# Source order on every engine, and a gate whose weight is the stationary operand

## The chip, the core and the metric

The kernel runs on one core of a Trainium2 chip. The metric is device time in microseconds (us) of one execution; before the change the median of three runs is 2077.51 us (2077.18 to 2080.61). Five engines work side by side, each through its own queue of instructions in the order in which the program was built: TensorE (PE, with its weight load shown as PEld), VectorE (DVE), ScalarE (ACT), GpSimd (POOL) and SyncE (SP), which here issues the DMAs. An engine that waits for a semaphore holds everything behind it in its queue.

## The reference

Three layers, one after the other, on 2304 tokens of 512 features:

```python
# attention: 4 batches, 8 heads, 576 positions, 64 features a head
q_s = exp(q - max(q, -1)); q_s /= sum(q_s, -1) + 1e-9
k_s = exp(k - max(k, 2));  k_s /= sum(k_s, 2) + 1e-9
x = (q_s @ (k_s^T @ v)).reshape(2304, 512)
# MLP: 512 -> 2048 -> 512
h = x @ w_in;  x = maximum(0.01 * h, h) @ w_out
# gate and Sinkhorn: 8 experts
P = exp(x @ w_gate - max)
for _ in range(8):
    P /= P.sum(1) + 1e-9;  P /= P.sum(0) + 1e-9;  P *= N / E
# dense mixture of experts, 512 -> 1024 -> 512 each
out = sum over e of P[:, e] * (maximum(x @ w1[e], 0) @ w2[e])
```

## The kernel before, in words

**Numbers.** Every fp32 product is emulated: an operand is split into a rounded part *hi* (a copy to fp32r on ACT) and a rest *lo* (a subtraction on DVE, or on POOL), and each product is three matmuls, hi·hi, hi·lo and lo·hi.

**MLP.** It runs in four phases of four hidden units of 128 each (`NPH`, `PU`); in a phase six blocks of 384 tokens (`NB`) pass, and each block takes the four units one after the other. That is 96 steps s. `first(s)` (L174) issues 12 matmuls into a bank `ph`, two leaky relus on ACT (`hh`, the hi part, L188, and `g`, L189) and on DVE the lo part of `hh` (L190). `second(s)` (L192) issues the 12 matmuls into the four `y` banks. At the end of a block the banks go into `acc` by four copies on ACT in phase 0 (L209), by four adds on DVE later (L211); the next block's first `y` matmul writes the same banks and waits for them. The pool of `hh` holds two tiles and that of `g` one, so that `hh` of step s+2 takes the tile that the `y` matmuls of step s read.

**Weights.** The MLP's weights arrive as 64 bit floats in half units of 512 KB (`raw`, three buffers) and `prep_half` (L126) turns each into hi and lo: an absolute value on ACT (L134), five integer and float operations on DVE (L136 to L146), a cast on ACT (L144), two operations on POOL (L148, L149); then it loads the next. The eight half units of a phase go to `wa` or to `wb_t` in turn.

**Gate.** After a block's last phase `gate_block` (L305) multiplies `acc` in plain fp32: 12 matmuls a block (24 in the trace) that hold a 128x128 piece of `acc` still and move the 8 columns of the gate's weight, into `pg`; a copy puts the logits into `lg`. `balance` (L320) takes the maximum (`pmx`, `pmb`) and runs the eight Sinkhorn rounds, each with one small matmul (`pcs`) between DVE operations (L336 to L347).

**Experts.** Three super-blocks of 768 tokens, 32 groups each, 96 groups. A group forms seven half-size products instead of eight (`pa` to `pd`, 6 matmuls each, L451) and then 36 matmuls of an earlier group's output (`e`, L464). `x_sums` (L418) prepares a super-block's seven sums of tokens on DVE and ACT, and splits them.

**What sets the order.** The source is a list of half steps: `half_step(t)` (L590) runs the tasks planned with `at(t, ...)`, advances those that are under way, then issues `first` or `second` (or a seventh of a group), then advances the tasks that asked for `PE_NEXT`. In the kernel before this is only the order of issue: the framework's scheduler then orders every engine's queue by its own estimate of what is ready, with the order of the source as a priority, and it may put a later step's operation ahead of an earlier one.

Of the kernel before, what the change touches and what calls it, by code (L numbers as in the profile page):

```python
# [15 lines left out]
P = 128  # L16
# [6 lines left out]
def kernel(  # L23
# [44 lines left out]
    US = 4 * DM  # L68
    HX = KC // 2 * BLK

    const = ctx.enter_context(tc.tile_pool(name="const", bufs=1))
    hp_ = ctx.enter_context(tc.tile_pool(name="h", bufs=2))
    sk_p = ctx.enter_context(tc.tile_pool(name="sk", bufs=2))
# [8 lines left out]
    def r32(ap):  # L82
        return ap.bitcast(F32)
# [82 lines left out]
    def bank(name):  # L166
        pool, tag = spare[0]
        spare.append(spare.pop(0))
        return pool.tile([P, 512], F32, tag=tag, name=name)
# [22 lines left out]
    def second(s):  # L192
        ph, b, u, beg, end = steps[s]
        if beg:
            for c in range(KC):
                y_t[c] = ps_y.tile([P, 512], F32, tag=f"y{c}", name=f"y{c}_{s}")[:, :BLK]
        assert (u, 1) in ready, (s, u)
        wh, wl = unit(u)[:, 1, 0, :], unit(u)[:, 1, 1, :]
        h = h_t.pop(s)
        for c in range(KC):  # L200
            cs = slice(c * P, (c + 1) * P)
            mm(y_t[c], wh[:, cs], h[:, 0, :], beg, False)
            mm(y_t[c], wh[:, cs], h[:, 1, :], False, False)
            mm(y_t[c], wl[:, cs], h[:, 0, :], False, end)
        if end:
            a = acc[b].rearrange("p (c n) -> p c n", c=KC)
            for c in range(KC):
                if ph == 0:
                    nc.scalar.copy(a[:, c, :], y_t[c])  # L209
                else:  # L210
                    nc.vector.tensor_tensor(a[:, c, :], y_t[c], a[:, c, :], op=ALU.add)  # L211
            if ph == NPH - 1:
                active.append([gate_block(b), PE_NEXT])


    k_t, v_t = {}, {}
# [85 lines left out]
        ready.add(("x", i))  # L302


    def gate_block(b):  # L305
        a = acc[b].rearrange("p (c n) -> p c n", c=KC)
        pg = bank(f"pg{b}")[:, : TB * E].rearrange("p (t e) -> p t e", e=E)
        for t in range(TB):
            for c in range(KC):
                mm(pg[:, t, :], a[:, c, t * P : (t + 1) * P], wg_t[:, c, :], c == 0, c == KC - 1)  # L310
        nc.scalar.copy(lg[:, b * TB : (b + 1) * TB, :], pg)
        ready.add(("gate", b))
        return
        yield

    mrow = const.tile([P, 1], F32, name="mrow")
    mall = const.tile([1, 1], F32, name="mall")
# [100 lines left out]
    def x_sums(sb):  # L418

        b = [  # L420
            acc[2 * sb + t].rearrange("p (k c n) -> p k c n", k=2, c=KC // 2)[:, k]
            for k in range(2)
            for t in range(2)
        ]
        b11, b12, b21, b22 = b
        t1 = later["mo"].tile([P, KC // 2, BLK], F32, tag="s", name=f"t1_{sb}", bufs=1)

        def sub(o, x, y):
            nc.vector.tensor_tensor(o, x, y, op=ALU.subtract)

        def both(name, a):
            split(xt(name)[:, 0], xt(name)[:, 1], a)()
            ready.add(("xt", sb, name))

        sub(t1, b12, b11)
        sub(b12, b22, b12)
        yield
        both("B11", b11)
        both("B22", b22)
        yield  # L440
        sub(b22, b22, t1)
        both("T2", b22)
        both("T1", t1)
        yield
        both("T3", b12)
        both("B21", b21)
        yield
        sub(b21, b21, b22)
        both("T4", b21)
# [211 lines left out]
    for ph in range(1, NPH - 1):  # L661
        for n, (f, half) in enumerate(halves):
            at(H2 * ph + 3 + 9 * n // 2, prep_half, PU * (ph + 1) + f, half)
    at(H2 * (NPH - 1) - 4, open_pairs)
    T3 = H2 * (NPH - 1)
    at(T3 + 8, pair0)
    at(T3 + 34, x_sums, 0)
    END = 2 * NS
    at(END + 2, balance)

    nc.vector.memset(ones, 1.0)
    nc.scalar.activation(mrow, ones[:, :1], AF.Exp)
# [74 lines left out]
```

## Time and profile before

| | |
|---|---|
| median of three runs | 2077.51 us |
| the profiled execution | 2077.42 us, with a span of 2075.6 us (1.82 us lie outside the span) |
| PE busy | 2024.7 us, 98% of the span |
| PEld, DVE, ACT, POOL busy | 1850.2, 1303.4, 794.1, 508.3 us |
| mean granted clock of PE | 0.987 of 2.4 GHz |
| attention and MLP | up to about 554 us |
| experts | about 554 to 2075.6 us, 15.7 us a group |

A page of the profile gives the busy time of each engine and the chain of work that ended last; its trace can be read as a timeline, by lines, by waits and by stretches of time. With PE at 98% the place to look is where PE is not busy, and where its clock is at the lower of its two levels (0.50 in the rows is 1.2 GHz).

### The profile page before, as it was taken

The page shows a single profiled execution, that of the slowest core. Times are in us where ns is not written, and L with a number is a line of the kernel's source. Part 1 is how long each engine was busy: PE and PEld are TensorE (multiplying, and loading weights), DVE is VectorE, ACT ScalarE, POOL GpSimd, SP SyncE. Part 2 cuts the span into 40 slices and gives each one's busy share as a digit, 9 for nine tenths or more (in the row PEclk, how much of TensorE's full clock was granted, in tenths as well). Part 3 has the DMA queues.
Part 4 walks back from the last instruction along what each step waited for, and adds up shares of the span by engine and source line. Part 5 has one row for each costly group of instructions (what it writes and reads, how often), then busy time and mean ns, then how long its engine had stood idle before and what let it go on. Part 6 is the DMA issues. An engine that isn't in the chain of part 4 may idle for free.

```text
span 2075.6 us, 26519 instructions
## 1 busy us (share of the span) xinstructions
PE 2024.7 (98%) x10447; PEld 1850.2 (89%) x10447; DVE 1303.4 (63%) x1899; ACT 794.1 (38%) x1342; POOL 508.3 (24%) x492
## 2 busy tenths in 40 slices
PE   7898798999999999999999999999999999999999
PEld 6898798999988988988988898898888889889887
DVE  8826826234486666666675666666676666666664
ACT  6644322223343343333344333343344433333431
POOL 5604404001121222222222212212212222222220
PEclk9999899999999999999999999999999999999999
DMA  6402202000121221221221211211213212212210
GB/s 239 151 7 74 89 3 89 1 1 1 42 81 41 82 82 41 82 82 41 82 97 57 81 64 59 82 56 67 82 41 112 81 41 81 82 41 82 82 41 31
DMA packets 65453, 138.57 MB, mean 67 GB/s; under 512 B 4656, under 2 KB 4656, under 8 KB 65328
## 3 DMA queue, kind: packets, MB, share of 16 engines
q1 hardware_dynamic: 65328, 136.87, 19.3%
q8 instruction: 82, 1.34, 0.3%
q14 instruction: 43, 0.35, 0.0%
HBM read 132.14 MB, written 4.72 MB: 66 GB/s over the span
## 4 chain that ended last, share of the span: by engine, by line
PE 86%; DVE 6%; issue 5%; ACT 1%; DMA 1%; POOL 1%; SPq 0%; POOLq 0%; ACTq 0%; DVEq 0%
PE e L172 38%; PE pa L172 9%; PE pc L172 9%; PE pd L172 9%; PE y L172 7%; PE ph L172 6%; PE pb L172 5%; DVE ca L140 1%; DVE ca L136 1%; DVE hh L190 1%; PE pg L172 1%; PE px L172 1%; DVE ca L137 1%; DVE raw L146 1%; PE pkv L172 1%
## 5 line engine op out<-in xcount | busy, mean ns | idle before, releaser
L172 PE MATMUL e<-wb_t,xs 128*128 128x512 f32 x3456 | 823.0, 395 | 0.2 <-DVE xs L498 0.2
L172 PEld LDWEIGHTS e<-wb_t,xs 128*128 128x128 f32 x3456 | 647.0, 188 | 149.6 <-DVE xs L498 0.7
L404 POOL TENSOR_TENSOR s<-pair 128x256 f32<-128x256 f32 x96 | 74.3, 774 | 1276.3 <-DMA pair<-in_w 703.8
L491 DVE SCALAR_TENSOR_TENSOR acc<-e,pm,acc 128x512 f32<-128x512 f32 x264 | 193.3, 745 | 104.9 <-PE e L172 102.3
L498 DVE SCALAR_TENSOR_TENSOR xs<-c,xs 128x384 fp32r<-128x384 f32 (+1 forms) x192 | 185.0, 982 | 84.2 <-ACT xs L497 81.1
L172 PE MATMUL pa<-xs,wa 128*128 128x384 f32 x1152 | 231.3, 335 | 2.2 <-ACT c L523 2.2
L172 PE MATMUL pc<-xs,wa 128*128 128x384 f32 x1152 | 230.8, 334 | 0.0
L172 PE MATMUL pd<-xs,wa 128*128 128x384 f32 x1152 | 230.6, 334 | 0.0
L497 ACT ACTIVATE xs<-c 128x768 fp32r<-128x768 f32 x192 | 126.6, 681 | 235.3 <-PE e L172 214.7
L172 PEld LDWEIGHTS pa<-xs,wa 128*128 128x128 f32 x1152 | 203.4, 188 | 11.5 <-ACT c L523 3.1
L172 PEld LDWEIGHTS pd<-xs,wa 128*128 128x128 f32 x1152 | 202.4, 188 | 0.0
L172 PEld LDWEIGHTS pc<-xs,wa 128*128 128x128 f32 x1152 | 202.3, 188 | 0.0
L190 DVE TENSOR_TENSOR hh<-g,hh 128x384 fp32r<-128x384 f32 x96 | 68.3, 712 | 187.6 <-ACT g L189 187.5
L398 DVE TENSOR_TENSOR wa<-s,wa 128x768 fp32r<-128x768 f32 x96 | 91.9, 957 | 105.0 <-ACT wa L397 102.8
L397 ACT CAST wa<-s 128x768 fp32r<-128x768 f32 x96 | 80.1, 835 | 174.4 <-POOL s L407 150.6
L513 DVE TENSOR_TENSOR c<-c 128x384 f32<-128x384 f32 x96 | 53.9, 562 | 135.3 <-ACT c L533 135.3
L172 PE MATMUL y<-hh,wa 128*128 128x384 f32 x576 | 119.8, 358 | 15.8 <-DVE acc L211 5.4
L172 PE MATMUL y<-hh,wb_t 128*128 128x384 f32 x576 | 118.6, 356 | 13.8 <-DVE hh L190 5.1
L523 ACT COPY c<-pa 128x384 f32<-128x384 f32 x96 | 46.2, 481 | 215.5 <-PE pa L172 164.9
L172 PEld LDWEIGHTS y<-hh,wa 128*128 128x128 f32 x576 | 108.0, 200 | 18.7 <-DVE hh L190 6.2
L172 PEld LDWEIGHTS y<-hh,wb_t 128*128 128x128 f32 x576 | 108.4, 202 | 16.6 <-DVE hh L190 6.4
L398 DVE TENSOR_TENSOR wa<-pair,wa 128x1024 fp32r<-128x1024 f32 x96 | 119.6, 1246 | 3.2 <-PE y L172 2.8
(106 smaller groups left out, 2515.5 us busy)
## 6 DMA issues: line engine op xcount, KB each, us to landing
pair<-in_w SPq DMA_DIRECT2D x192, 512.0 KB, 4.9
raw<-in_wm SPq DMA_DIRECT2D x32, 512.0 KB, 3.8
v<-in_vt SPq DMA_DIRECT2D x16, 320.0 KB, 4.7
k<-in_kt SPq DMA_DIRECT2D x16, 288.0 KB, 4.2
out<-acc SPq DMA_DIRECT2D x18, 256.0 KB, 2.0
acc<-in_q SPq DMA_DIRECT2D x5, 768.0 KB, 5.9
acc<-in_q SPq DMA_DIRECT2D x3, 256.0 KB, 5.2
wg_t<-in_wg SPq DMA_DIRECT2D x1, 16.0 KB, 8.9
```

Of the source, the lines that this page charges most:

```text
L136: nc.vector.tensor_scalar(af, af, EXP_MIN, EXP_MAX, op0=ALU.max, op1=ALU.min)
L137: nc.vector.tensor_scalar(a, a, 3, 0x3FFFFFFF, op0=ALU.logical_shift_left, op1=ALU.bitwise_and)
L172: nc.tensor.matmul(o, a, b, start=start, stop=stop, **more)
L190: nc.vector.tensor_tensor(hh[:, 1, :], g, r32(hh[:, 0, :]), op=ALU.subtract)
L397: nc.scalar.copy(hi, a)
L398: return lambda: nc.vector.tensor_tensor(lo, a, r32(hi), op=ALU.subtract)
L404: nc.gpsimd.tensor_tensor(s[:, 0], a21, a22, op=ALU.add)
L491: nc.vector.scalar_tensor_tensor(a, y, scale, a, op0=ALU.mult, op1=ALU.add)
L497: nc.scalar.activation(o[:, 0], p, AF.Relu)
L498: nc.vector.scalar_tensor_tensor(o[:, 1], p, 0.0, r32(o[:, 0]), op0=ALU.max, op1=ALU.subtract)
L513: add = lambda o, x, y: nc.vector.tensor_tensor(o, x, y, op=ALU.add)
L523: nc.scalar.copy(c1, bk[0])
```

## The change

There are four edits. The scheduler is switched off, so that every engine's queue is in the order of the source (`manual_schedule`). The gate is turned round: `acc` is split into hi and lo (into the part of `xs` that held the attention's result for that block, which no one reads any more), the weight becomes the stationary operand with its hi and lo parts side by side (16 columns, `wgs`), 8 matmuls move 384 tokens each into a 16x384 result `pg`, which is split again (`gs`, hi on ACT, lo on DVE), and six small matmuls with `sel`, two identity blocks summed, turn it back to tokens by experts (`pt`) and add the two halves of the weight. The first temporary of `x_sums` takes a tile of the pool `hh` for super-blocks 1 and 2. `balance` starts three half steps later. Line numbers of the kernel after are higher by 2 up to the gate, by 30 to 31 behind it.

```diff
--- before.py
+++ after.py
@@ -68,6 +68,8 @@
     US = 4 * DM
     HX = KC // 2 * BLK
 
+
+    ctx.enter_context(tc.manual_schedule())
     const = ctx.enter_context(tc.tile_pool(name="const", bufs=1))
     hp_ = ctx.enter_context(tc.tile_pool(name="h", bufs=2))
     sk_p = ctx.enter_context(tc.tile_pool(name="sk", bufs=2))
@@ -210,7 +212,7 @@
                 else:
                     nc.vector.tensor_tensor(a[:, c, :], y_t[c], a[:, c, :], op=ALU.add)
             if ph == NPH - 1:
-                active.append([gate_block(b), PE_NEXT])
+                active.append([gate_block(b), None])
 
 
     k_t, v_t = {}, {}
@@ -302,16 +304,44 @@
         ready.add(("x", i))
 
 
+
+    gx = wa[:, PU * US - 2 * DM :]
+    wgs = gx[:, : KC * 2 * E].rearrange("p (c e) -> p c e", c=KC)
+    sel = gx[: 2 * E, KC * 2 * E :][:, :E]
+    gs = gx[: 2 * E, -2 * BLK :].rearrange("p (l n) -> p l n", l=2)
+
+    def gate_weight():
+
+
+        nc.scalar.copy(wgs[:, :, :E], wg_t)
+        nc.vector.tensor_tensor(wgs[:, :, E:], wg_t, r32(wgs[:, :, :E]), op=ALU.subtract)
+        nc.vector.tensor_tensor(
+            sel, ident[: 2 * E, :E], ident[: 2 * E, E : 2 * E], op=ALU.add
+        )
+
     def gate_block(b):
-        a = acc[b].rearrange("p (c n) -> p c n", c=KC)
-        pg = bank(f"pg{b}")[:, : TB * E].rearrange("p (t e) -> p t e", e=E)
+
+        for k in range(2):
+            ks = slice(k * XS // 2, (k + 1) * XS // 2)
+            hi, lo = (xs[:, (2 * b + l) * XS : (2 * b + l + 1) * XS][:, ks] for l in range(2))
+            nc.scalar.copy(hi, acc[b][:, ks])
+            nc.vector.tensor_tensor(lo, acc[b][:, ks], r32(hi), op=ALU.subtract)
+            if k == 0:
+                yield
+        yield PE_NEXT
+        pg = bank(f"pg{b}")[: 2 * E, :BLK]
+        for c in range(KC):
+            for l in range(2):
+                mm(pg, wgs[:, c, :], xb(b, l)[:, c, :], c + l == 0, c + l == KC)
+        nc.scalar.copy(gs[:, 0], pg)
+        nc.vector.tensor_tensor(gs[:, 1], pg, r32(gs[:, 0]), op=ALU.subtract)
+        yield PE_NEXT
+        pt = bank(f"pt{b}")[:, : TB * E].rearrange("p (t e) -> p t e", e=E)
         for t in range(TB):
-            for c in range(KC):
-                mm(pg[:, t, :], a[:, c, t * P : (t + 1) * P], wg_t[:, c, :], c == 0, c == KC - 1)
-        nc.scalar.copy(lg[:, b * TB : (b + 1) * TB, :], pg)
+            for l in range(2):
+                mm(pt[:, t, :], gs[:, l, t * P : (t + 1) * P], sel, l == 0, l == 1)
+        nc.scalar.copy(lg[:, b * TB : (b + 1) * TB, :], pt)
         ready.add(("gate", b))
-        return
-        yield
 
     mrow = const.tile([P, 1], F32, name="mrow")
     mall = const.tile([1, 1], F32, name="mall")
@@ -423,7 +453,8 @@
             for t in range(2)
         ]
         b11, b12, b21, b22 = b
-        t1 = later["mo"].tile([P, KC // 2, BLK], F32, tag="s", name=f"t1_{sb}", bufs=1)
+        pool, tag, bufs = (hp_, "hh", 2) if sb else (later["mo"], "s", 1)
+        t1 = pool.tile([P, KC // 2, BLK], F32, tag=tag, name=f"t1_{sb}", bufs=bufs)
 
         def sub(o, x, y):
             nc.vector.tensor_tensor(o, x, y, op=ALU.subtract)
@@ -662,11 +693,12 @@
         for n, (f, half) in enumerate(halves):
             at(H2 * ph + 3 + 9 * n // 2, prep_half, PU * (ph + 1) + f, half)
     at(H2 * (NPH - 1) - 4, open_pairs)
+    at(H2 * (NPH - 1) + 2, gate_weight)
     T3 = H2 * (NPH - 1)
     at(T3 + 8, pair0)
     at(T3 + 34, x_sums, 0)
     END = 2 * NS
-    at(END + 2, balance)
+    at(END + 5, balance)
 
     nc.vector.memset(ones, 1.0)
     nc.scalar.activation(mrow, ones[:, :1], AF.Exp)
```

On PE at the first gate, before: `ph78` is the first matmul of step 78, `y0_76` to `y3_76` the banks of the block that begins at step 76.

```order
L172 MATMUL ph78_3864<-xs_81,wb_t_1680 128x384 x12
L172 MATMUL pg0_3882<-wg_t_72,acc0_75 128x8 x12
L172 MATMUL y0_76_3897<-hh76_3808,wb_t_1680 128x384 x3
L172 MATMUL y1_76_3898<-hh76_3808,wb_t_1680 128x384 x3
L172 MATMUL y2_76_3899<-hh76_3808,wb_t_1680 128x384 x3
L172 MATMUL y3_76_3900<-hh76_3808,wb_t_1680 128x384 x3
L172 MATMUL ph79_3915<-xs_81,wb_t_1680 128x384 x12
L172 MATMUL y0_76_3897<-hh77_3838,wb_t_1680 128x384 x3
L172 MATMUL y1_76_3898<-hh77_3838,wb_t_1680 128x384 x3
```

And of the kernel after, same place on PE:

```order
L174 MATMUL ph79_3910<-xs_83,wb_t_1682 128x384 x12
L174 MATMUL pg0_3928<-xs_83,wa_84 16x384 x8
L174 MATMUL y0_76_3892<-hh77_3843,wb_t_1682 128x384 x3
L174 MATMUL y1_76_3893<-hh77_3843,wb_t_1682 128x384 x3
L174 MATMUL y2_76_3894<-hh77_3843,wb_t_1682 128x384 x3
L174 MATMUL y3_76_3895<-hh77_3843,wb_t_1682 128x384 x3
L174 MATMUL pt0_3952<-wa_84 128x8 x6
L174 MATMUL ph80_3960<-xs_83,wb_t_1682 128x384 x12
```

`pg0` still stands between a `ph` and a `y`, one step later, with 8 matmuls of 384 columns for 12 of 8; behind the next `y` come the six `pt0` matmuls, ahead of `ph80`.

What stands on ACT there in the kernel after (`wa<-pg0` is the hi part of the gate's result):

```order
L427 CAST wa_84<-pair0_3663 128x1024
L427 CAST wa_84<-s0_3866 128x768
L190 ACTIVATE hh79_3923<-ph79_3910 128x384
L191 ACTIVATE g79_3924<-ph79_3910 128x384
L336 CAST wa_84<-pg0_3928 16x384
L343 COPY lg_75<-pt0_3952 128x24
L190 ACTIVATE hh80_3973<-ph80_3960 128x384
L191 ACTIVATE g80_3974<-ph80_3960 128x384
```

The split of `pg0` stands behind `hh79` and `g79`, and the copy of the logits behind it.

On ACT at the end of block 5 of phase 0, before, where `acc5<-y..` are the copies that free the `y` banks and `ca` is the first operation of a half unit's preparation:

```order
L188 ACTIVATE hh24_1913<-ph24_1900 128x384
L189 ACTIVATE g24_1914<-ph24_1900 128x384
L134 ACTIVATE ca8_1_2215<-raw8_1_2031 128x512
L134 ACTIVATE ca10_0_2291<-raw10_0_2103 128x512
L209 COPY acc5_80<-y0_20_1834 128x384
L209 COPY acc5_80<-y1_20_1835 128x384
L144 CAST wa_82<-ca8_1_2215 128x512
L209 COPY acc5_80<-y2_20_1836 128x384
L188 ACTIVATE hh25_1959<-ph25_1946 128x384
L189 ACTIVATE g25_1960<-ph25_1946 128x384
L209 COPY acc5_80<-y3_20_1837 128x384
L144 CAST wa_82<-ca10_0_2291 128x512
```

And after:

```order
L146 CAST wb_t_1682<-ca7_0_1882 128x512
L136 ACTIVATE ca6_1_1927<-raw6_1_1877 128x512
L190 ACTIVATE hh25_1961<-ph25_1948 128x384
L191 ACTIVATE g25_1962<-ph25_1948 128x384
L146 CAST wb_t_1682<-ca6_1_1927 128x512
L136 ACTIVATE ca7_1_1969<-raw7_1_1922 128x512
L211 COPY acc5_82<-y0_20_1836 128x384
L211 COPY acc5_82<-y1_20_1837 128x384
L211 COPY acc5_82<-y2_20_1838 128x384
L211 COPY acc5_82<-y3_20_1839 128x384
L190 ACTIVATE hh26_2007<-ph26_1994 128x384
L191 ACTIVATE g26_2008<-ph26_1994 128x384
```

The preparations of phase 2's half units (`ca8` to `ca10`), which stood ahead of and between the copies, are gone from here; the copies now stand behind `ca7_1`, in one piece, ahead of `hh26`.

On DVE at the end of super-block 0, before (`t1_1` and the operations on `acc2`, `acc3` belong to `x_sums`, `wa<-s32` prepares group 32, `c1_31` and `c2_31` are sums of group 31):

```order
L398 TENSOR_TENSOR wa_82<-s32_8273,wa_82 128x768
L498 SCALAR_TENSOR_TENSOR xs_81<-c1_30_8152,xs_81 128x384
L498 SCALAR_TENSOR_TENSOR xs_81<-c2_30_8151,xs_81 128x768
L491 SCALAR_TENSOR_TENSOR acc0_75<-e14_0_8220,pm_74,acc0_75 128x512
L429 TENSOR_TENSOR t1_1_8328<-acc3_78,acc2_77 128x768
L398 TENSOR_TENSOR wa_82<-pair32_8207,wa_82 128x1024
L491 SCALAR_TENSOR_TENSOR acc0_75<-e14_1_8236,pm_74,acc0_75 128x512
L429 TENSOR_TENSOR acc3_78<-acc3_78 128x768
L491 SCALAR_TENSOR_TENSOR acc0_75<-e14_2_8251,pm_74,acc0_75 128x512
L513 TENSOR_TENSOR c1_31_8270<-pb_31_8266,c1_31_8270 128x384
L398 TENSOR_TENSOR xs_81<-acc2_77,xs_81 128x768
L398 TENSOR_TENSOR xs_81<-t1_1_8328,xs_81 128x768
```

And after:

```order
L460 TENSOR_TENSOR acc3_80<-acc3_80 128x768
L544 TENSOR_TENSOR c1_31_8329<-pd_31_8327,c1_31_8329 128x384
L529 SCALAR_TENSOR_TENSOR xs_83<-c1_31_8329,xs_83 128x384
L428 TENSOR_TENSOR xs_83<-acc2_79,xs_83 128x768
L428 TENSOR_TENSOR xs_83<-acc3_80,xs_83 128x768
L522 SCALAR_TENSOR_TENSOR acc1_78<-e14_3_8404,pm_76,acc1_78 128x512
L428 TENSOR_TENSOR wa_84<-pair32_8266,wa_84 128x1024
L460 TENSOR_TENSOR acc3_80<-acc3_80,t1_1_8387 128x768
L428 TENSOR_TENSOR xs_83<-acc3_80,xs_83 128x768
L428 TENSOR_TENSOR xs_83<-t1_1_8387,xs_83 128x768
L522 SCALAR_TENSOR_TENSOR acc1_78<-e14_4_8425,pm_76,acc1_78 128x512
L428 TENSOR_TENSOR wa_84<-s32_8332,wa_84 128x768
```

`wa<-s32`, the last of what group 32's second product reads, stands ahead of all of `x_sums` before. After, it stands behind seven of the operations of `x_sums` (the first, `t1_1`, is in the row ahead of those shown) and behind `wa<-pair32`.

## Rows read from the trace of the kernel before

**Rows 1.** Stretches of the span: length, busy us (instructions) by engine, clock, DMA.

```profile
core 0: us, PE busy (x) PEld busy (x) DVE busy (x) ACT busy (x) POOL busy (x), PEclk, DMA share, GB/s
0.00:67.10 67.10, 53.81 (x305) 48.28 (x305) 60.26 (x107) 43.61 (x98) 42.55 (x39) 0.90 0.65 224
67.10:110.90 43.80, 38.93 (x231) 36.89 (x230) 33.59 (x89) 28.36 (x66) 21.97 (x21) 0.92 0.40 127
...
174.12:249.25 75.13, 57.26 (x265) 54.22 (x265) 69.78 (x87) 29.62 (x59) 44.76 (x30) 0.86 0.35 113
...
320.80:342.07 21.27, 14.72 (x73) 13.78 (x73) 20.40 (x26) 6.60 (x13) 11.97 (x9) 0.92 0.39 124
...
553.95:619.40 65.45, 62.80 (x336) 56.05 (x336) 54.77 (x119) 29.24 (x48) 18.62 (x17) 1.00 0.23 76
619.40:2046.55 1427.15, 1425.30 (x7090) 1275.67 (x7090) 948.51 (x1288) 554.51 (x841) 343.60 (x356) 1.00 0.20 68
```

**Rows 2.** Timeline of PE, 183 to 345 us: start, length; in brackets idle before, releaser.

```profile
187.65 3.91 PE L172 MATMUL y<-hh,wa 128*128 128x384 f32 x12 [2.81 <-ACT acc L209]
...
214.66 1.79 PE L172 MATMUL y<-hh,wb_t 128*128 128x384 f32 x6 [3.80 <-ACT acc L209]
...
245.60 3.85 PE L172 MATMUL y<-hh,wb_t 128*128 128x384 f32 x12 [4.02 <-DVE acc L211]
...
338.49 3.75 PE L172 MATMUL y<-hh,wa 128*128 128x384 f32 x12 [5.35 <-DVE acc L211]
```

**Rows 3.** Short stretches, columns as in rows 1; the sixth number is the clock.

```profile
215.28:222.11 6.83, 5.92 (x18) 5.09 (x18) 6.80 (x11) 4.13 (x9) 4.52 (x3) 0.50 0.27 84
227.40:228.30 0.90, 0.04 (x2) 0.03 (x1) 0.90 (x2) 0.00 (x0) 0.82 (x2) 1.00 0.17 68
...
461.04:464.45 3.41, 3.41 (x12) 3.41 (x12) 0.00 (x0) 0.14 (x1) 0.00 (x0) 0.50 0.00 0
```

**Rows 4.** Chain that ended last, at the first gate: start, length, what.

```profile
458.39 2.58 PE pg L172 x24
460.96 3.75 PE y L172 x12
464.71 2.08 PE ph L172 x12
```

**Rows 5.** Timeline of all engines just ahead of the first gate.

```profile
454.02 2.25 PE L172 MATMUL y<-hh,wb_t 128*128 128x384 f32 x12
...
454.75 2.12 DVE L211 TENSOR_TENSOR acc<-y,acc 128x384 f32<-128x384 f32 x4 [1.18 <-PE y L172]
...
456.60 0.48 ACT L188 ACTIVATE hh<-ph 128x384 fp32r<-128x384 f32 x1
...
456.98 0.49 ACT L189 ACTIVATE g<-ph 128x384 f32<-128x384 f32 x1
457.64 0.55 DVE L190 TENSOR_TENSOR hh<-g,hh 128x384 fp32r<-128x384 f32 x1
```

**Rows 6.** Waits of the whole run: us in total, times, longest.

```profile
ACT hh L188 <- PE y L172: 178.3, 62, 3.6
```

**Rows 7.** Instructions by line: busy us, mean ns; idle before, releaser.

```profile
L491 DVE SCALAR_TENSOR_TENSOR acc<-e,pm,acc 128x512 f32<-128x512 f32 x264 | 193.3, 745 | 104.9 <-PE e L172 102.3
...
L398 DVE TENSOR_TENSOR wa<-pair,wa 128x1024 fp32r<-128x1024 f32 x96 | 119.6, 1246 | 3.2 <-PE y L172 2.8
...
L513 DVE TENSOR_TENSOR c<-pb,c 128x384 f32<-128x384 f32 x96 | 53.3, 555 | 48.4 <-PE pb L172 48.4
...
L398 DVE TENSOR_TENSOR xs<-acc,xs 128x768 fp32r<-128x768 f32 x18 | 17.5, 984 | 1.4 <-PE ph L172 1.2
```

**Rows 8.** Chain that ended last, at the end of super-block 0.

```profile
1037.48 1.04 PE pa L172 x6
...
1040.60 8.40 PE e L172 x36
...
1057.51 4.67 PE e L172 x20
```

## The prediction

> **What bounds the kernel now.** I read the stretches first: their PE column shows where PE is not full. From 619 us on it is full, 1425.3 of 1427.2 us at full clock [rows 1], so the experts are bound by PE and source order can only lose there. What can be gained lies in four earlier stretches: PE is busy for 53.8 of 67.1 us, 38.9 of 43.8, 57.3 of 75.1 and 14.7 of 21.3, each with a clock under 1 [rows 1]. A pair of `ph` and `y` costs 4.2 us at full clock (12 matmuls in 2.08 us [rows 4], twice). The 265 matmuls of the third stretch are 11 pairs or 46.3 us, so 28.8 of its 75.1 us are lost; the 73 of the fourth are 3 pairs or 12.6 us, so 8.7 are lost. Next the timeline of PE says what ended the idle time: the copies and adds that free the `y` banks [rows 2], on engines that were then preparing weights (DVE is busy for 69.8 of the 75.1 us [rows 1]). Last I read the clock. The 3.80 us of idle are followed by 6.8 us at 1.2 GHz, whereas at 227.4 us PE is idle for 0.9 us and stays at 2.4 [rows 3]. Twelve matmuls at the lower level took 3.75 us for 2.08 [rows 4], so each drop costs 1.7.
>
> **The change part by part** (after minus before, against the profiled execution's 2077.42 us: a span of 2075.6 and 1.82 outside it; the median of the runs is 2077.51, 0.09 more).
>
> *Start, 0 to 110.9 us.* DVE is busy for 60.3 of the first 67.1 us [rows 1], and its operations there are needed in either order. But the scheduler also does work of the following 44 us early, preparations and softmax pieces. Source order leaves them in their place, so PE should fill 67 to 111 (4.9 us of idle and about 3.5 of lost clock to win, 8% of 43.8). Against that, the first `ph` comes 3 to 6 us later, since pieces of later tasks stand on DVE ahead of the last operation that it needs. I take −5, from −12 to +5.
>
> *111 to 174 us.* PE is full there before; source order brings a few short stalls: +1 (0 to +5).
>
> *Phase 0 to 1, 174 to 249 us.* The scheduler brings phase 2's preparations forward into this stretch, back to back with phase 1's. After, only the eight of phase 1 stand there, some two half steps apart. Two waits remain. The copies of block 4's banks stand on ACT behind `hh21` and a cast that waits for DVE: about 1.9 us. Those of block 5 stand behind `ca7_1`, which waits for a load that in turn waits for POOL to free a buffer: about 5.9. With one to three drops of the clock at 1.7, 9.5 to 13 us are lost for 28.8. That is −17; if nothing waits for loads −24, if more blocks do −8.
>
> *Phases 1 to 3 up to the gate, 249 to 458 us.* The 8.7 us of 321 to 342 go with the crowd of preparations. New is that a block's four adds, 2.12 us on DVE [rows 5], stand behind the lo part of the next `hh` and a preparation's operations; before, they ran ahead of it. The next block's `y` then waits 1.3 us in one block and 2.0 in another of each of phases 1 and 2 (6.6), fourteen other blocks about 0.17 (2.4), and a drop of the clock may follow: +1 (−3 to +5).
>
> *Gate.* Before, a block's gate is 2.58 us on PE [rows 4]. After, eight matmuls of 384 columns at 2.08/12 = 0.173 take 1.4 and the six of `pt` some 0.6 (at 2.58/24 each), 2.0 altogether: 0.6 less, if nobody waits. But `pt0` reads `gs`, whose split stands on ACT behind `hh79` and `g79`. `hh79` takes the tile that `y` of step 77 reads, so it starts only when that `y` has ended. The timeline shows just this wait before: `y` starts at 454.02, takes 2.25, and `hh` starts at 456.60, 0.33 behind its end [rows 5]; ACT spends 178 us so in all [rows 6]. Behind `pg0` PE has just that `y`, and then `pt0`: from the end of `y`, 0.33 for `hh`, 0.87 to `g`'s end (456.60 to 457.47 [rows 5]), about 0.4 for the split's hi, 0.5 for its lo and 0.6 for `pt`: 2.7 us in which PE does next to nothing. A block costs 1.4 + 2.7 = 4.1 for 2.58, so five blocks lose 7.6; the sixth stands among the experts. Lost clock is worth 4.6 in all before (three of six `y` behind a gate are slow, the first with 3.75 [rows 4]); after, each wait of some 2 us may bring 1.7, 0 to 8.5 in all, and I take the same as before. Together +7.6 (+2.6 to +12).
>
> *Balance, 554 to 619 us.* Before, PE is idle for 2.65 us there [rows 1], since the scheduler slides the expert matmuls under each step of the chain. After, the eleven small matmuls (`pt5`, `pmx`, `pmb` and eight `pcs`) have fixed places. The longest waits: `pmx` stands behind a maximum that waits on ACT for `lg`, itself behind a relu and a cast, 2.8; `pcs1` behind a DVE row with one 1.25 and several 0.55 operations of the group [rows 7] and the round's own, 5.9; five more of 0.3 to 1.4, 3.6 together. 12.3 us and two drops of the clock at 1.7 give 15.7, less 2.65 is 13.0; the second drop is unsure, and I take +12 (+7 to +16).
>
> *Ends of super-blocks 0 and 1.* A group is 7 × 1.04 + 8.40 = 15.68 us [rows 8]; at the first end 16.91 pass between two equal points, 1040.60 to 1057.51 [rows 8], so 1.2 are lost. After, from `t1_1` to `wa<-s32` DVE has eight operations of about 0.97, one of 1.25, two of 0.75 and two of 0.55 [rows 7]: 11.6 us, less a little overlap, from some 9.6 us into group 31 on (its four sums and `wb_t<-pair31` come first). So `wa<-s32` is there at 21.1, and the second product of group 32, which would end at 15.68 + 2 × 1.04 = 17.8, ends at 21.9. The splits that follow, T4 last, hold the copy that frees bank `pa` until about 26.4; three more products then end at 29.5 for 23.0. That is 6.5 less 1.2, or 5.3, and up to 8.7 with two drops of the clock; 7 each, +14 (+10 to +18).
>
> *Steady groups, tail.* Walked in source order, DVE and ACT (948.5 and 554.5 of 1427 us [rows 1]) have what PE needs in time: 0.
>
> Sum: −5 + 1 − 17 + 1 + 7.6 + 12 + 14 = +13.6, so 2091.0 us.
>
> **A rule on the clock.** The rows show drops behind idle of 3.80 us and none behind 0.9 [rows 3], and one behind the gate's matmuls without idle [rows 4]. The Trainium skill ("TensorE: Matmul & The Clock Gate", "A second HAM failure mode: psum-queue depth-cycling") says that frequent short idles of TensorE between groups of matmuls can be enough to make the clock swing. The trace agrees only in part: no drop stands at the 0.9 us. By that rule the many short waits that source order adds would cost clock too, which is the third rival.
>
> **The rivals.**
> 1. *Faster: preparations spread over the half steps stall nobody.* It decides in 174 to 249 us: if loads arrive ahead of `ca7_1`, the stretch loses under 5 us, −24 for −17, and with the start at −12 and 249 to 458 at −3, the same mechanism, the first half gives −38. Against the costs at their middle, 7.6 + 12 + 14 = 33.6, that is −4 (2073); at their lower ends, 19.6, −18 (2059). For it: the idle there is crowding, DVE 93% busy [rows 1]. Against: `ca7_1`'s wait stands ahead of the bank's copies in the order. I put it at 2066.
> 2. *Cancelled: the gate's wait doesn't occur.* If `gs` is split before `y` of step 77 ends, five blocks give 5 × 0.6 = 3.0, and the 4.6 of clock may go too: −5 in place of +7.6, the sum is +1.0, and the time 2078 (2071 with balance and the ends of super-blocks near their lower ends as well). For it: `pg0` is done early. Against: two `hh` tiles and the row of 178 us [rows 6].
> 3. *Much slower: every wait of 1 us or more takes the clock down.* About 14 waits (four in phases 1 and 2, five at the gate, five in balance) at 1.7 are 24 us, of which 8 are in the sum (4.6 at the gate, 3.4 in balance): +30, or 2107. For it: the slow `y` behind the gate without idle [rows 4]. Against: 227.4 us [rows 3].
>
> **How the numbers follow.** The forecast's own range, its terms not all at one end, is 2082 to 2103, with a chance of 0.48. The first rival has 0.22, the second 0.16, the third 0.14. A time within 0.2% (4.2 us, about what a measurement of this kernel can tell) of 2077.5 is no change. Faster: 0.20 of the first rival and 0.04 of the second, 0.24. Same: 0.02 and 0.11, 0.13. Slower: the rest, 0.63. The range is 2063 to 2109, with about a tenth beyond each end.
>
> **What would show it.** Right: in the new profile PE's idle before `y` between 174 and 249 us is cut to a few us; `pt` has 2 us of idle ahead of it in five blocks, released by DVE; `pcs` and `pmx` have idle ahead in the first four groups; two groups are some 6 us longer than 15.68. Wrong: the first `ph` more than 8 us later than before, or earlier than it, a steady group unlike 15.68 us, no idle ahead of `pt`, or a mean clock under 0.98.

## The result, and the profile after

The kernel after takes 2102.44 us (median of four runs, 2099.86 to 2104.33) against 2078.03 beside it: slower, with a ratio of 1.0109 (95% interval 1.0095 to 1.0122). Its profiled execution has a span of 2100.8 us, 25.2 more than before. The prediction was 2091.0 us within 2063 to 2109: the right side and within the range, but 13.6 us forecast for the 24 measured.

The stretches of the kernel after, with the columns of [rows 1]; cut at the first matmul of steps 8 and 20, inside steps 32 and 77, at the first group and at the seventh:

```profile
0.00:102.50 102.50, 81.75 (x496) 74.53 (x496) 74.78 (x133) 57.81 (x135) 46.82 (x44) 0.90 0.54 187
102.50:175.13 72.63, 70.19 (x453) 68.17 (x453) 30.09 (x65) 37.69 (x87) 16.88 (x16) 1.00 0.06 21
175.13:240.94 65.81, 56.91 (x298) 55.98 (x298) 46.36 (x67) 25.80 (x55) 30.70 (x20) 0.90 0.25 73
240.94:439.07 198.13, 192.22 (x1082) 189.03 (x1081) 82.64 (x162) 54.78 (x119) 46.27 (x32) 1.00 0.14 43
439.07:552.01 112.94, 102.63 (x544) 95.91 (x542) 45.99 (x71) 34.09 (x68) 3.12 (x4) 0.94 0.00 1
552.01:649.80 97.79, 88.26 (x437) 78.12 (x436) 71.25 (x144) 39.92 (x65) 17.85 (x23) 0.95 0.20 65
```

PE idles for 10.3 us in the fifth and 9.5 in the sixth. Before, it was full at the gate, and 2.65 us were idle in the first groups [rows 1]. Lengths of the same work in both kernels, from the starts of the same matmuls on PE's timeline (`pb` of groups 0, 6, 30, 34, 62 and 66 for the experts); the predicted terms are for nearly these stretches, cut at 110.9, 174, 249 and 458 us of the kernel before:

| stretch | before | after | measured | predicted |
|---|---|---|---|---|
| start to `ph` of step 8 | 104.5 | 102.5 | −2.0 | −5 |
| to `ph` of step 20 | 69.6 | 72.6 | +3.0 | +1 |
| to `ph` of step 33 | 83.6 | 68.5 | −15.1 | −17 |
| to `ph` of step 78 | 198.4 | 198.1 | −0.3 | +1 |
| gate, to group 0 | 98.9 | 111.3 | +12.4 | +7.6 |
| balance, to group 6 | 87.2 | 96.7 | +9.5 | +12 |
| two ends of super-blocks | 127.9 | 145.4 | +17.5 | +14 |
| 24 steady groups, 6 to 30 | 376.3 | 376.3 | 0 | 0 |

PE's timeline in the kernel after, where it waits: the two block ends of phase 0 (compare [rows 2]), the first gate, the maximum, the second round's sum, and the end of super-block 0.

```profile
188.13 3.91 PE L174 MATMUL y<-hh,wa 128*128 128x384 f32 x12 [2.27 <-ACT acc L211]
...
213.45 4.21 PE L174 MATMUL y<-hh,wb_t 128*128 128x384 f32 x12 [6.62 <-ACT acc L211]
...
453.24 0.27 PE L174 MATMUL pt<-wa 16*128 16x8 f32 x1 [1.30 <-ACT wa L336]
453.95 0.71 PE L174 MATMUL pt<-wa 16*128 16x8 f32 x5 [0.44 <-DVE wa L337]
454.59 3.90 PE L174 MATMUL ph<-xs,wb_t 128*128 128x384 f32 x12
...
535.61 2.32 PE L174 MATMUL y<-hh,wb_t 128*128 128x384 f32 x12 [1.60 <-DVE acc L213]
...
564.46 0.37 PE L354 MATMUL pmx<-ident,mrow 128*1 128x128 f32 x1 [2.75 <-DVE mrow L351]
...
579.93 0.59 PE L174 MATMUL pcs<-cs,ones 128*128 128x8 f32 x2 [5.57 <-DVE cs L370]
...
1057.39 0.96 PE L174 MATMUL pa<-xs,wa 128*128 128x384 f32 x4 [0.44 <-DVE wa L428]
1059.12 0.45 PE L174 MATMUL pb<-xs,wa 128*128 128x384 f32 x1 [0.77 <-ACT xs L427]
1060.12 0.44 PE L174 MATMUL pb<-xs,wa 128*128 128x384 f32 x1 [0.55 <-DVE xs L428]
1062.51 1.65 PE L174 MATMUL pb<-xs,wa 128*128 128x384 f32 x4 [1.95 <-DVE wa L428]
...
1068.91 2.25 PE L174 MATMUL pa<-xs,wa 128*128 128x384 f32 x6 [1.96 <-ACT c L554]
```

The waits stand where the order of the engines put them. What precedes `pt` on the other engines, after `y` (449.69, 2.25 long):

```profile
451.98 0.49 ACT L190 ACTIVATE hh<-ph 128x384 fp32r<-128x384 f32 x1 [2.32 <-PE y L174]
452.36 0.48 ACT L191 ACTIVATE g<-ph 128x384 f32<-128x384 f32 x1
452.73 0.45 ACT L336 CAST wa<-pg 16x384 fp32r<-16x384 f32 x1
452.88 0.56 DVE L192 TENSOR_TENSOR hh<-g,hh 128x384 fp32r<-128x384 f32 x1 [2.70 <-ACT g L191]
...
453.36 0.54 DVE L337 TENSOR_TENSOR wa<-pg,wa 16x384 fp32r<-16x384 f32 x1
```

ACT is idle for 2.32 us, its queue held by the `hh` that waits for `y`, while `pg` has been there to be split.

### The profile page after: what moved, and what is told of

Same layout as the page of the kernel before. It is cut to its first block, busy times and chain, and to the rows that moved or that the text cites. A ratio compares the mean times of both kernels' runs of the same rounds, so it can differ in the third digit from the quotient of the medians.

```text
span 2100.8 us, 26261 instructions
## 1 busy us (share of the span) xinstructions
PE 2027.9 (97%) x10387; PEld 1843.2 (88%) x10387; DVE 1295.8 (62%) x1919; ACT 785.1 (37%) x1361; POOL 471.7 (22%) x492
## 4 chain that ended last, share of the span: by engine, by line
PE 90%; DVE 6%; ACT 2%; issue 1%; DMA 0%; POOL 0%; SPq 0%; ACTq 0%; POOLq 0%
PE e L174 37%; PE pa L174 9%; PE y L174 9%; PE pc L174 9%; PE pd L174 9%; PE ph L174 8%; PE pb L174 5%; PE px L174 1%; DVE ca L138 1%; PE pkv L174 1%; DVE xs L428 1%; DVE hh L192 1%; DVE ca L139 1%; PE pg L174 0%; ACT hh L190 0%
## 5 line engine op out<-in xcount | busy, mean ns | idle before, releaser
L522 DVE SCALAR_TENSOR_TENSOR acc<-e,pm,acc 128x512 f32<-128x512 f32 x264 | 198.3, 751 | 213.2 <-PE e L174 213.0
L528 ACT ACTIVATE xs<-c 128x384 fp32r<-128x384 f32 x192 | 131.4, 685 | 402.3 <-DVE c L544 266.8
L529 DVE SCALAR_TENSOR_TENSOR xs<-c,xs 128x384 fp32r<-128x384 f32 x192 | 174.0, 906 | 79.5 <-ACT xs L528 79.5
L174 PEld LDWEIGHTS pa<-xs,wa 128*128 128x128 f32 x1152 | 206.1, 190 | 14.6 <-ACT c L554 4.4
L192 DVE TENSOR_TENSOR hh<-g,hh 128x384 fp32r<-128x384 f32 x96 | 56.4, 588 | 224.8 <-ACT g L191 224.7
L190 ACT ACTIVATE hh<-ph 128x384 fp32r<-128x384 f32 x96 | 47.1, 490 | 231.5 <-PE y L174 215.9
L174 PE MATMUL pb<-xs,wa 128*128 128x384 f32 x576 | 119.1, 340 | 6.5 <-DVE wa L428 3.9
L174 PE MATMUL y<-hh,wb_t 128*128 128x384 f32 x576 | 113.5, 347 | 10.9 <-ACT acc L211 6.6
L437 POOL TENSOR_TENSOR s<-pair,s 128x256 f32<-128x256 f32 x96 | 122.1, 1272 | 7.5
L174 PE MATMUL ph<-xs,wa 128*128 128x384 f32 x576 | 112.5, 344 | 6.8 <-DVE xs L303 5.4
L174 PE MATMUL y<-hh,wa 128*128 128x384 f32 x576 | 112.6, 345 | 5.5 <-DVE acc L213 3.2
```

The source lines that it names most:

```text
L174: nc.tensor.matmul(o, a, b, start=start, stop=stop, **more)
L190: nc.scalar.activation(hh[:, 0, :], p, AF.Prelu, alpha=0.01)
L192: nc.vector.tensor_tensor(hh[:, 1, :], g, r32(hh[:, 0, :]), op=ALU.subtract)
L437: nc.gpsimd.tensor_tensor(s[:, 2], a12, s[:, 1], op=ALU.subtract)
L522: nc.vector.scalar_tensor_tensor(a, y, scale, a, op0=ALU.mult, op1=ALU.add)
L528: nc.scalar.activation(o[:, 0], p, AF.Relu)
```

## The experiments

All were timed against the kernel before on the same chip (medians there 2078.6 to 2081.0 us). Line numbers shift by a few.

**Source order alone.** Two edits to the kernel before:

```diff
+    ctx.enter_context(tc.manual_schedule())
-        t1 = later["mo"].tile(..., tag="s", name=f"t1_{sb}", bufs=1)
+        pool, tag, bufs = (hp_, "hh", 2) if sb else (later["mo"], "s", 1)
+        t1 = pool.tile(..., tag=tag, name=f"t1_{sb}", bufs=bufs)
```

> The kernel before with its old gate and balance where it was, in source order on every engine (with the first temporary of x_sums in the pool of hh, without which source order cannot finish). My theory: the loss of the gate section (11 us by the two traces) comes from the new gate's second small product, pt, waiting behind y in source order, and the old gate has no such second product; so source order alone costs about 25 - 11 = 14 us over before: some 2092 us (2087 to 2097), with the gains in 174 to 458 us, the balance's and the super-blocks' losses all still there. Rival: the loss at the gate is source order's whatever the gate, and this kernel takes about 2102 us like the kernel after.

2105.85 us, ratio 1.0119 (1.0100 to 1.0138). The theory fell: the old gate in source order loses 16.5 us in its stretch (`ph` of step 78 starts 14.6 us ahead of before, group 0 1.9 behind), more than the new one's 12.4 (the 11 us of the expectation are cut inside step 77). On PE's timeline:

```profile
443.72 4.40 PE L173 MATMUL pg<-wg_t,acc 128*128 128x8 f32 x24
...
537.48 5.31 PE L173 MATMUL pg<-wg_t,acc 128*128 128x8 f32 x24 [4.31 <-DVE acc L212]
```

The order, then, carries the whole loss, and the new gate softens it.

**The other edits alone.** `manual_schedule` taken out of the kernel after.

> The kernel after with the scheduler left on: the other three edits alone. My theory: the scheduler slides another ph ahead of pt, nothing waits for gs, and the gate gets 0.5 us a block cheaper with less lost clock: 2070 to 2078 us, median about 2075, with no idle over 0.5 us before pt. Rival: the new gate is dearer in itself, by its chain of split, product, split, product or by narrow matmuls that take the clock down: 2083 to 2090 us.

2069.02 us, 0.9946 (0.9931 to 0.9961): faster than before. The gate's stretch is 5.8 us shorter than before (93.1 for 98.9), the ends of super-blocks take 62.72 us, 4 × 15.68, with nothing lost. ACT, DVE and PE at the first gate:

```profile
463.54 1.55 PE L173 MATMUL pg<-xs,wa 128*16 128x384 f32 x8
...
465.12 0.47 ACT L335 CAST wa<-pg 16x384 fp32r<-16x384 f32 x1
466.00 0.54 DVE L336 TENSOR_TENSOR wa<-pg,wa 16x384 fp32r<-16x384 f32 x1
...
467.10 0.83 PE L173 MATMUL pt<-wa 16*128 16x8 f32 x6
467.21 0.49 ACT L189 ACTIVATE hh<-ph 128x384 fp32r<-128x384 f32 x1 [1.62 <-PE y L173]
```

On PE the order at this place is the one of the kernel after; on ACT the scheduler has put the split ahead of `hh`, and `pt` waits for nothing.

**`pt` half a step later.**

```diff
         nc.vector.tensor_tensor(gs[:, 1], pg, r32(gs[:, 0]), op=ALU.subtract)
+        yield
         yield PE_NEXT
```

> The kernel after with pt one half step later, behind the next ph (one more yield). My theory: the 2.0 us without PE work ahead of and inside pt in each of five blocks go (9 us), and with the idle time the four drops of the clock behind it (1.7 us each, 6.8): 15 us less than the kernel after, about 2087 us (2084 to 2091). Rival: the drops of the clock come from the narrow matmuls of pg and pt and not from idle time; then only about 9 us are gained, 2093 us, and the ph or y behind pt still take 3.4 to 3.9 us.

2093.05 us, 1.0065 (1.0045 to 1.0084): 9.4 less than the kernel after. The gate's stretch is 10.2 us shorter (101.1 for 111.3). In the first four blocks the idle time and the slow `ph` behind it are gone; in the fifth `pt` still waits 1.74 us. Block 4 gave part back: its wait of 1.60 us became 3.71, with a slow `y` behind.

```profile
453.11 0.83 PE L174 MATMUL pt<-wa 16*128 16x8 f32 x6
453.87 2.37 PE L174 MATMUL y<-hh,wb_t 128*128 128x384 f32 x12
...
524.50 3.88 PE L174 MATMUL y<-hh,wb_t 128*128 128x384 f32 x12 [3.71 <-DVE acc L213]
```

Ahead of those adds on DVE stand a last subtraction and split of `x_sums`. The size is thus the rival's (2093), but the rival's sign, slow matmuls behind `pt` with no idle, is not there: in the four blocks where the edit took hold the theory's mechanism is seen, and the fifth and the adds account for what is short.

**`pg` ahead of `ph`.**

```diff
             if k == 0:
                 yield
-        yield PE_NEXT
+        yield
         pg = bank(f"pg{b}")[: 2 * E, :BLK]
```

> The kernel after with pg one place earlier, ahead of ph instead of behind it, so that the split of pg stands ahead of hh and g on ScalarE; pt stays where it is, right behind y. My theory: pt waited because the split stood behind an hh that waits for y; now the split is done while ph runs, pt has no wait, and some 15 us are gained as with pt later: about 2087 us (2083 to 2092). Rival: pt waits because the chain split, pg, split, pt is itself longer than the one step that it is given; then pg or pt waits 1 us or more still and under 6 us are gained, over 2096 us.

2101.18 us, 1.0101 (1.0084 to 1.0118). `pt` has no wait, as the theory has it, but `pg` now waits 1.6 us for the split of `acc`, as the rival has it:

```profile
447.42 0.35 PE L174 MATMUL pg<-xs,wa 128*16 128x384 f32 x1 [0.98 <-ACT xs L327]
448.41 0.70 PE L174 MATMUL pg<-xs,wa 128*16 128x384 f32 x3 [0.64 <-DVE xs L328]
...
453.20 0.83 PE L174 MATMUL pt<-wa 16*128 16x8 f32 x6
```

The chain split, `pg`, split, `pt` doesn't fit into the steps that source order gives it, and block 4's adds hold `y` for 3.42 us here. That no `pt` waits shows, as the scheduled version does, that the split's place behind `hh` was the cause.

**The last half unit later.**

```diff
-    ... zip((35, 36, 38, 40, 42, 43, 45, 47), halves):
+    ... zip((35, 36, 38, 40, 42, 43, 45, 50), halves):
```

> The kernel after with the last half unit of phase 1 prepared three half steps later (50 for 47), so that its first operation on ScalarE, which waits for a load, stands behind the copies of block 5's banks and not ahead of them. My theory: the 6.6 us that PE waits before y of step 24 shrink to about 1, and with them 2 us of lost clock behind: about 8 us less than the kernel after, 2094 us (2092 to 2098). Rival: the wait only moves on, to the hh that stands behind this load's wait; then under 3 us are gained and a new idle time of 3 us or more stands before a y or ph between 214 and 240 us.

2102.63 us, 1.0111 (1.0096 to 1.0126): nothing gained, the wait is 7.60 us. Both theories fell. What stands ahead of the copies on ACT is a cast that waits for DVE:

```profile
206.81 0.62 ACT L146 CAST wb_t<-ca 128x512 fp32r<-128x512 f32 x1 [3.41 <-DVE ca L142]
...
211.92 0.62 ACT L146 CAST wb_t<-ca 128x512 fp32r<-128x512 f32 x1 [3.18 <-DVE ca L142]
212.45 1.61 ACT L211 COPY acc<-y 128x384 f32<-128x384 f32 x4
```

In the kernel after, too, `ca7_1` (`ca<-raw`) follows on that cast without a wait for its load:

```profile
211.85 0.62 ACT L146 CAST wb_t<-ca 128x512 fp32r<-128x512 f32 x1 [3.16 <-DVE ca L142]
...
212.38 0.66 ACT L136 ACTIVATE ca<-raw 128x512 f32<-128x512 f32 x1
```

**Preparations without GpSimd.**

```diff
-        nc.gpsimd.tensor_tensor(af, af, r32(hi), op=ALU.subtract)
-        nc.gpsimd.tensor_tensor(lo, af, ef, op=ALU.add)
+        nc.vector.tensor_tensor(af, af, r32(hi), op=ALU.subtract)
+        nc.vector.tensor_tensor(lo, af, ef, op=ALU.add)
```

> The kernel after with the last two operations of each half unit's preparation on VectorE in place of GpSimd. My theory, from the run with the last half unit later, which changed nothing: the wait of 6.6 us before y of step 24 is VectorE's rate. In the trace a preparation takes 5.4 us on VectorE there, of which the first two operations take 1.4 to 1.5 us beside GpSimd and 0.43 alone. With GpSimd idle VectorE has two more operations of about 0.7 but none that is stretched: about 4.2 us each. Then the wait before y of step 24 falls under 2 us, the first ph pairs start some us earlier too (eight preparations there), and the time is about 2090 us (2085 to 2096). Rival: VectorE is the bound, and 1.4 us more per preparation make it later: 2105 us or more, with longer idle before y of steps 20 and 24.

2101.94 us, 1.0098 (1.0075 to 1.0121): theory and rival both fell. First a row of the kernel after, with GpSimd busy beside it:

```profile
208.16 1.49 DVE L138 TENSOR_SCALAR ca<-ca 128x512 f32<-128x512 f32 x1
```

and then of this kernel:

```profile
207.96 0.42 DVE L138 TENSOR_SCALAR ca<-ca 128x512 f32<-128x512 f32 x1
...
211.23 4.21 PE L174 MATMUL y<-hh,wb_t 128*128 128x384 f32 x12 [7.20 <-ACT acc L211]
```

The stretched operations are short now (1.49 to 0.42), DVE does two more, and the wait before `y` of step 24 stays (7.20 for 6.62). The Trainium skill (SBUF — State Buffer, "SBUF: two separate sides") has VectorE and GpSimd share one pair of ports under an exclusive lock; the trace agrees with 1.49 us beside GpSimd and 0.42 without. But the lock does not decide this wait: DVE's queue is without a gap either way. Something was gained all the same: the wait before `y` of step 20 is gone (0.17 for 2.27 us), and from step 20 to step 33 pass 65.3 us for 68.5. It is lost again behind: 2.0 us up to step 78, and 3.9 at the gate, where block 4's adds hold `y` for 2.62 us and not 1.60 and the clock falls behind it.

**Balance slower and later.**

```diff
-    at(END + 5, balance)
+    at(END + 8, balance)
             nc.vector.tensor_reduce(cs, pm.rearrange("p t e -> p e t"), ...)
+            yield
             yield PE_NEXT
```

(and the same `yield` behind the first maximum)

> The kernel after with balance three half steps later (END + 8) and one half step more between each sum on VectorE and the small matmul that reads it. My theory: the idle times before pmx (2.75 us) and pcs (5.57 and some of 0.3) go, and with them the drops of the clock behind; from the first group to the seventh 88 us in place of 96.8: some 8.5 us less, 2094 us (2091 to 2098). Rival: these stretches are bound by the splits of the first groups' weights on VectorE and ScalarE, which have no e matmuls to hide behind, and the small matmuls only happen to stand there; then the idle time appears before pa, pb or e in their place, and under 3 us are gained.

2092.56 us, 1.0067 (1.0050 to 1.0084), 9.9 less, within the theory's range. In the stretch itself 5.9 us went (90.8 for 96.7) and not the theory's 8.8; the waits of 2.75 and 5.57 us are gone, but `pa` now waits 1.28 us for a weight's split, the rival's sign, and a wait of 2.66 before `pmb` is new:

```profile
570.59 0.38 PE L174 MATMUL pmb<-mall,ones 1*128 1x1 f32 x2 [2.66 <-DVE mall L356]
```

Most of the rest stands ahead of the edit, in drops of the clock that this execution didn't have at the gate (one behind the five `pt`, four in the kernel after): the size came in part by luck.

**The sums of a super-block earlier.** `x_sums` from the second half step of the last group, not the fourth; the split of B11 in its first piece, then one empty half step, and the rest in other pieces, over six half steps instead of five. The sums of super-block 0 have the same pieces.

```diff
         sub(t1, b12, b11)
         sub(b12, b22, b12)
-        yield
         both("B11", b11)
+        yield
+        yield
         both("B22", b22)
...
-            at(t + 3, x_sums, i // NQ + 1)
+            at(t + 1, x_sums, i // NQ + 1)
```

> The kernel after with the sums of the next super-block begun two half steps earlier (at the second of the last group, the first split there too) and handed out one piece at a time over six half steps. My theory: the two boundaries lose 10.0 us each because twelve operations of VectorE stand ahead of the weight split that the next group's second product reads; with four of them ahead earlier and the rest thinner 3 to 4 us are lost each: about 12 us less, 2090 us (2087 to 2095). Rival: VectorE is simply full there (9.6 us of sums beside 9.3 us of the group in 15.7 us), and the loss only moves to other products of the two groups: under 5 us gained, 2097 or more.

2098.56 us, 1.0095 (1.0080 to 1.0110): 3.9 less, the rival's size. But the two ends lose 6.2 and 4.9 us for 10.0 each, 8.9 less together, about three quarters of the theory's 12; PE now waits in front of `pa`:

```profile
1067.70 1.65 PE L174 MATMUL pa<-xs,wa 128*128 128x384 f32 x4 [2.69 <-DVE wa L428]
```

In the profiled execution, the longest of the four, 6.2 us are lost again at the gate (117.5 for 111.3), where the sums of super-block 0 now hold block 4's adds for 3.50 us in place of 1.60, with a slow `y` and `ph` behind. The small total is thus no sign that the ends only moved their loss.

**The sums in another order** (T2 built in the temporary, B21, B22 and T4 only in the next group; begun at the second half step, and for super-block 0 four half steps later):

```diff
+        sub(t1, b22, t1)
+        both("T2", t1)
...
+        both("B21", b21)
+        sub(b21, b21, t1)
+        yield
+        both("B22", b22)
```

> The kernel after with x_sums alone in that other order: before the weight split of group 32 stand two subtractions and the split of B11, then T1, then one subtraction and T2; T3 behind the splits of group 32's weights; B21, B22 and T4 in group 32. My theory: the loss of 10.0 us at a boundary is the place of x_sums ahead of the weight's splits on VectorE and ScalarE; now 0 to 3 us are left at each: 14 to 20 us less than the kernel after and 2 more at block 4's adds, 2085 us (2081 to 2089). Rival: VectorE is full in these groups whatever the order; 5 us or more stay at each boundary, 2091 or more.

2107.64 us, 1.0129 (1.0108 to 1.0151): nothing gained on the kernel after; 10.2 us are lost at each end. The same order in the second combination shows where: `pb` waits 1.1 us, but `pc` 2.3 and `pd` 2.5 for the splits that now come late:

```profile
1039.49 0.98 PE L174 MATMUL pb<-xs,wa 128*128 128x384 f32 x4 [1.13 <-DVE wa L433]
...
1044.81 0.44 PE L174 MATMUL pc<-xs,wa 128*128 128x384 f32 x1 [1.07 <-ACT xs L432]
1046.47 1.14 PE L174 MATMUL pc<-xs,wa 128*128 128x384 f32 x5 [1.23 <-DVE xs L433]
...
1050.26 1.97 PE L174 MATMUL pd<-xs,wa 128*128 128x384 f32 x5 [2.47 <-DVE xs L433]
```

**Two combinations.**

The first: the edits of `pt` later, the last half unit later, balance, and the sums earlier, and

```diff
-    at(T3 + 34, x_sums, 0)
+    at(T3 + 40, x_sums, 0)
```

> All of these together with pt later, and x_sums of super-block 0 six half steps later (so that its 4.6 us on VectorE no longer stand ahead of the adds that free block 4's banks). My theory: the terms add up, as they stand in separate stretches: 2102 less 9 to 11 (pt), 4 (block 4's adds), 8 (last half unit), 8.5 (balance), 12 (boundaries) gives 2060 us (2056 to 2068), faster than the kernel before by 0.5 to 1% and than the new gate under the scheduler (2069). Rival: source order has one loss for another; what is taken away comes back as waits elsewhere, and the sum is over 2075 us.

2081.05 us, 1.0006 (0.9997 to 1.0015).

The second keeps balance as in the first; it has the sums in the other order and the preparations without GpSimd, the last half unit where it was, and

```diff
         nc.vector.tensor_tensor(gs[:, 1], pg, ...)
+        yield
+        yield
         yield PE_NEXT
...
         nc.vector.tensor_reduce(mall, pt, ...)
+        yield
         yield PE_NEXT
...
-    at(T3 + 34, x_sums, 0)
+    at(T3 + 38, x_sums, 0)
```

> All together, revised: pt two half steps later, balance from END + 8 with a half step more at each sum and at the maximum, x_sums in another order (T2 built in the temporary, so that B22, B21 and T4 are split only in the first half steps of the next group) and for super-block 0 from four half steps later, and the preparations' last two operations on VectorE. My theory: from the 2081 us of the first combination 12 go at the boundaries, about 10 with the preparations, 3 at balance and the last pt: 2056 us (2050 to 2064), faster than both kernels. Rival: losses move on as in the first combination, where 21 us of some 43 came: 2068 us or more.

2081.60 us, 1.0007 (0.9995 to 1.0019). Both are equal to before: 21 us of the 24 are back, and both rivals hold: at the ends of super-blocks 6.9 and some 10 us stay lost.

**Source order up to phase 3, the scheduler behind it.**

```diff
-    ctx.enter_context(tc.manual_schedule())
+    man = ExitStack()
+    man.enter_context(tc.manual_schedule())
...
     for s in range(NS):
+        if s == SP * (NPH - 1):
+            man.close()
```

> The kernel after in source order for phases 0 to 2 of the MLP alone; the scheduler orders everything from the first step of phase 3 on (the context of source order is closed there). My theory: source order gains 13 us up to 452 us, in the two stretches where the scheduler crowds preparations, and loses all it loses behind that, 38 us, where the scheduler alone is 11 us faster than before (2069 with the new gate). The two parts stand in separate stretches and add: 2078 - 13 - 11 = 2054 us (2050 to 2059), faster than the kernel before, after and the scheduled new gate. Rival: the gain of the first part is given back, since the scheduler's gain in phase 3 rests on work that it had done before it; then 2063 to 2070 us.

2053.05 us, 0.9870 (0.9853 to 0.9886), within 1 us of the theory's 2054 and faster than every other kernel here. Its stretches at the gate, balance and the end of super-block 0:

```profile
438.00:533.00 95.00, 95.00 (x545) 89.99 (x544) 50.17 (x72) 37.03 (x70) 9.19 (x8) 1.00 0.06 17
533.00:620.25 87.25, 84.91 (x438) 75.06 (x437) 73.28 (x149) 40.11 (x64) 20.70 (x21) 1.00 0.16 56
996.57:1059.29 62.72, 62.72 (x314) 56.15 (x314) 50.57 (x69) 28.89 (x44) 15.41 (x16) 1.00 0.25 88
```

PE is full at the gate (93.1 us from `ph` of step 78 to group 0, for 111.3); four groups over the end of a super-block take 62.72. `ph` of step 78 starts 15.0 us ahead of before (14.4 in the kernel after). So source order is worth some 15 us up to the gate, and behind it costs 49: from `ph` of step 78 to the last matmul 1606.3 us here, as in the scheduled new gate, and 1655.2 in the kernel after.

## Why the prediction was right, and what its sum missed

- **Side and structure: right.** Each term of the sum lies in its own range but the gate's, 0.4 us beyond it, and each has its sign but that of phases 1 to 3 (−0.3 for +1). The last experiment shows gain and loss to be separate: one kept, the other left, and the time is their sum. The misses stand mostly on one side (start and 111 to 174 us +5, gate +4.8, ends +3.5, phase 0 to 1 +1.9, against balance −2.5 and phases 1 to 3 −1.3), so the sum came out at little more than half of the change, and the range held it.
- **Gate: mechanism right, size short (+12.4 for +7.6).** A block's `pt` ends 2.8 us behind `y` (2.7 predicted), 8.0 us in five blocks, held by the `hh` that waits for `y`; with the split ahead of that `hh` on ACT, in the scheduled version and with `pg` ahead of `ph`, `pt` has no wait. Short was the term "the same as before" for the clock: the `ph` or `y` behind `pt` runs slow in four of five blocks, 3.90 us for 2.1 at the first, about 2 us more than before in all. And two waits were not in the sum: 1.60 us at block 4's adds, behind `x_sums` of super-block 0 on DVE, and some 0.2 us before one `y` in each of the other four.
- **Ends of super-blocks: mechanism right, size short (+17.5 for +14).** Some 10.0 us are lost at each for the 6.5 and "up to two drops": the idle rows above add to 5.7 us, and two stretches of 3.5 us, from 1062.5 and 1068.9 us, run near 1.2 GHz (clock 0.56 and 0.51), about 3.3 us more. It isn't VectorE's sum of work alone: the scheduler does the same work with no loss. In source order ACT and DVE wait for each other in turn there:

```profile
1058.24 0.83 ACT L427 CAST xs<-acc 128x768 fp32r<-128x768 f32 x1 [3.09 <-DVE acc L460]
...
1059.11 0.96 DVE L428 TENSOR_TENSOR xs<-acc,xs 128x768 fp32r<-128x768 f32 x1 [0.90 <-ACT xs L427]
...
1066.92 0.83 ACT L427 CAST xs<-acc 128x768 fp32r<-128x768 f32 x1 [5.65 <-DVE acc L460]
```

Beginning the sums earlier took back 3.8 and 5.1 us of the two ends; the other order took back none and moved the wait to other products. Which order on DVE and ACT loses nothing is not shown apart from the scheduler's.

- **Phase 0 to 1: size right (−15.1 for −17), mechanism wrong in one step.** The step that failed is "those of block 5 stand behind `ca7_1`, which waits for a load". `ca7_1` has no wait of its own in the kernel after (212.38), and with it behind the copies the wait stayed (7.60 us). The copies stand behind a cast, and that waits for DVE, where preparations come 4.8 to 5.1 us apart against 4.2 for a pair on PE. Neither a later last half unit nor an idle GpSimd took this wait away; what would is not shown.
- **Start and 111 to 174 us: too hopeful by 5 together.** Of the 8.4 us to win between 67 and 111 us some came, but the first `ph` comes 3.1 us later and then waits 5.1 us for DVE behind its first matmul, and two `px` after 111 us wait 1.0 and 1.4.
- **Balance: too dark (+9.5 for +12).** The long waits are those forecast, 2.75 (2.8) and 5.57 us (5.9); the smaller ones of 0.3 to 1.4 us were 0.2 to 0.3.
- **The rivals.** The second, a gate without a wait, is what the scheduler makes of the same gate: 5.8 us less. The third, every wait takes the clock down, is half true: none of the four waits of 1.06 to 1.53 us before `y` in phases 1 and 2 did. By the Trainium skill's rule on short idles ("TensorE: Matmul & The Clock Gate", "A second HAM failure mode: psum-queue depth-cycling") the clock might have fallen there too; the trace shows it at full level (clock 1.00 from 240.94 to 439.07 us).

## What to carry to other kernels

A global order needn't be chosen for the whole program: read, stretch by stretch, whether a scheduler's reordering hides work or crowds it, and keep source order only where it crowds. In source order, look for any operation that stands on an in-order engine behind one that waits for the very engine that will need it; here one such place on ScalarE left TensorE idle for 1.74 us in each of five blocks. When one edit's wait is removed and the time stays, read what the next instruction in the queue waits for before moving the same thing again.

## What was unexpected of the hardware

- The clock behind similar idle times differs from run to run. `y` behind 2.27 us of idle took 3.91 us in the kernel after, and 2.39 in the last experiment at the same place; what follows `pt`, behind 1.74 us of idle, was slow in four of five blocks, and in the run with balance slower, whose gate is the same, in one. With `pg` ahead of `ph` 1.62 us of idle before `pg`, in two parts, left the next `ph` at full speed in all five. Behind 6 us and more `y` took 3.8 to 4.2 in every run with source order there. The drop behind the 2.27 us cost nothing: in the last experiment the next wait was longer (8.13 for 6.62 us), and the `y` behind it began at the same time (213.23 and 213.45), since the copies came no sooner.

```profile
187.92 2.39 PE L175 MATMUL y<-hh,wa 128*128 128x384 f32 x12 [2.27 <-ACT acc L212]
...
213.23 4.21 PE L175 MATMUL y<-hh,wb_t 128*128 128x384 f32 x12 [8.13 <-ACT acc L212]
```

- The old gate's 24 matmuls of 8 columns, without idle around them, were followed by a slow `y` in three of the five blocks in which a `y` follows (the first in [rows 4]); eight of 384 columns and six of 8, without idle, by none in the first four blocks of the run with `pt` later. The clock lost before was worth 4.6 us, and without waits the new gate is 0.44 us a block shorter (1.38 from `pg` to `y` and 0.76 from `pt` to `y` there, for 2.58), 2.2 for five: 6.8 together, where the scheduled version gains 5.8.
